# Attention and a routed expert layer on one core: when the first expert's weights are loaded and split, and at which steps two closings hand work to GpSimd

## The chip, the cores and the metric

The kernel runs on one core of a Trainium2 chip. The metric is the device time of one execution in microseconds (us). Engines are called by the profile's short names: PE (TensorE, matrix products), PEld (its weight loads), DVE (VectorE), ACT (ScalarE), POOL (GpSimd) and SP (SyncE, which only issues transfers here). Each engine works its own queue in program order and waits at semaphores for the others.

## The reference

The program computes an attention whose queries and keys may only meet inside the same hash bucket, and sends its result through a layer of eight experts:

```
x = bucket_attention(q, k, v, proj)            # 4 batches, 8 heads, 768 tokens, 64 wide -> 3072 tokens x 512
logits = x @ w_gate                            # 3072 x 8
for (token, e) in all pairs, highest logit first:
    if token is free and expert e has fewer than 384 tokens: assign it
for e in range(8):
    h = max(x[tokens of e] @ w1[e], 0)         # 384 x 512  by  512 x 1024
    out[tokens of e] = h @ w2[e]               # 384 x 1024 by 1024 x 512
```

The greedy assignment is done in rounds: each round finds which expert fills up next, and which 384 tokens it has. Such a round is a **closing**. There are eight; each yields one expert's tokens and the row numbers of its weights.

## The kernel before, in words

**Stages.** The first part (some 410 us) is the attention. Then closing 0 runs alone. From there on expert k's two matrix products run on PE while closing k+1 is worked in between, mostly on DVE, with short products on PE.

**Precision.** A weight or a token block is split into a high part (ACT copies it to a rounded format, `wh`, `xh`) and a low part (the difference, `wl`, `xl`). A product is three passes: high by high, weights' low by high, and high by the other low. So a weight piece is loaded by DMA to `wf`, copied by ACT to `wh` (L731), and subtracted by POOL to `wl` in two instructions of 128x512 (L743). A weight of an expert is four such pieces, so eight subtractions; both weights of an expert need sixteen. `wf`, `wh`, `wl` of each layer exist once.

**Steps.** `run` (L818) writes the expert part in 68 steps per expert. Steps 0 to 31 are the first layer: eight blocks `f` of four steps, three products of 384 columns to a step (L777), with ACT's `hh` (L779) and DVE's `hl` (L780) at the end of a block. Block f uses weight piece f//2, the low part from its fifth product on. Steps 32 to 67 are the second layer: three blocks `c` of twelve steps, two products of 512 columns to a step (L789); the last eight products of a block use `wl`, piece by piece, so that the second half of piece 3 is read by the last product of the block, in its last step (43 for the first block). Before a step, `run` emits what is planned for it: steps of the closing, splits of weights (`wsplit`, L725) and of tokens (`xsplit`, four times), loads, scatters of results. A step is only a place in each engine's program order; each engine reaches it at its own time. Steps of expert k are counted from 68k here and told from the expert's own step 0.

**Closings.** A closing is a generator (`phase`, L546), advanced at planned steps: lists E1 for closing 1 (over expert 0) and E2 for closing 2 (over expert 1), EV for the others. In E1 the entries are steps -12, -4, -3, 2, 6, 7, 8, 14, 20, 27, 33, 36, 39, 46; in E2 -9, -8, -6, 1, 8, 15, 20, 23, 27, 38, which is 59 to 106 counted from the start of expert 0. In order: the best logits and a compare; a count on PE and a threshold (L593 to L605); five more rounds of count (L518), threshold (L605 makes `d2`) and compare (L500); the outcome (L611 to L638, PE L614, L641); the member lists (L649, L677, L662 makes `cc`); the collection of the row numbers on PE (L651), and the update (L667 to L675). With the row numbers POOL gathers the tokens (`gather`, L709) by indirect DMA, and `wload` (L716) the weights.

**Hand-outs.** For experts 0 to 5 the subtractions of POOL are not emitted where the split is planned but put on a list (`pend`), with a step by which they must be emitted at the latest. At each closing step `step(p,n)` advances the closing, and `hand(n)` (L739) emits the next n of them behind a `tick` (L737), a copy of one element of the closing's latest result, so that POOL starts them only when DVE has got that far. The lists `hs` in `run` say how many at each closing step.

**Start.** `start` (L802) loads two pieces of expert 0's first weight, ends closing 0, gathers the tokens, splits pieces 0 and 1 (with DVE for the low parts) and the tokens. Then a tick on POOL waits for the tokens' split; behind it POOL issues the loads of pieces 2 and 3 and of the second weight in two halves. Their splits are planned in `run`: pieces 2 and 3 before steps 4 and 6 (`W10`), the second weight's before steps 9, 12, 15, 18 (`W20`).

Of the kernel before, what the change touches and what calls it, by code (L numbers as in the profile page):

```python
# [42 lines left out]
def attention(tc, nc, ctx, qT, kT, vv, proj, wg, x_dram, L, jp, identf, B, late=None, after=None):  # L43
# [322 lines left out]
    for t in range(6*NH+LAG+6):  # L366
        h,s=divmod(t,6)
        first=(t-LAG)%6==5
        if first: av(t)
        if t<6*NH and t not in early: ST(h,s,0)  # L370
        for x in S_at.get(t,[]): S_pass(*x)
        run(2*t)
        if h<NH: ST(h,s,1)
        if t>=1 and (t-1)//6<NH:
            hh,ss=divmod(t-1,6)
            lo(hh,ss,V if ss in (E0 if hh<1 else E1 if hh<2 else PAT[hh%2]) or t==6*NH else G_)
        run(2*t+1)
        if not first: av(t)
# [14 lines left out]
HS=[0,3,3,2,3,3,0,0,2,0]  # L393
BY=[-1,8,36]
W2=[2,4,7,11]
W10=[(2,4),(3,6)]
W20=[9,12,15,18]
XS=[57,57,60,63]
XS1=[61,61,64,65]
KW=[1,0,4,0,2,19,7,1]  # L400
# [1 line left out]
class Moe:  # L402
# [399 lines left out]
    def start(s):  # L802

        s.ps0=None; V=s.nc.vector
        s.wload(0,0,4,(0,1))
        next(s.ph0)
        s.gather(0)
        s.wsplit(0,0,0,V)
        next(s.ph0)
        s.ch=[s.phase(p) for p in range(8)]  # L810
        s.wsplit(0,0,1,V)
        s.xsplit0()

        s.gate=s.W[0,'x'][0][0:1,0,256:257].bitcast(F32); s.tick()
        s.wload(0,0,4,(2,3))
        s.wload(0,1,2)

    def run(s):  # L818
        V=s.nc.vector; ch=s.ch; at={}; NS=68
        def add(n,f,*a): at.setdefault(n,[]).append((f,a))  # L820
        def end(p):
            s.gather(p)
            if p<7: next(ch[p+1])
        def step(p,n):
            next(ch[p],None); s.hand(n)
        for p in range(1,8):
            b=NS*(p-1)
            ev=[b+e for e in (E1 if p==1 else E2 if p==2 else EV)]
            dec=ev[-3] if p<7 else ev[-2]-2
            hs=[0]*(len(ev)-10)+HS  # L830
            if p==1: hs=[0,0,0,0,0,2,2,2,2,2,0,1,1,0]
            if p==2: hs=[0,2,3,2,3,2,0,0,4,0]
            if p==7: ev=ev[-2:]; hs=[0,0]
            for e,n in zip(ev,hs): add(e,step,p,n)
            add(ev[-1],end,p)
            add(max(dec,b+WL[0]),s.wload,p,0); add(max(ev[-1],b+WL[1]),s.wload,p,1)
            for q in range(4):
                add(b+(W11 if p==1 else W1)[q],s.wsplit,p,0,q,None,b+NS+BY[0]+BY[1]*q if p<6 else 0)
                add(b+(XS1 if p==1 else XS)[q],s.xsplit,p,q)
        for k in range(8):  # L840
            for q in range(4): add(NS*k+(W2 if k else W20)[q],s.wsplit,k,1,q,None,NS*k+(BY[2] if k else 42) if k<6 else 0)
            for n in SC: add(NS*k+n,s.scatter)
        for q,n in W10: add(n,s.wsplit,0,0,q,None,8*q-2)
        for n in range(-NS,NS*8):
            for f,a in at.get(n,()): f(*a)
            while s.pend and s.pend[0][0]<=n: s.nc.gpsimd.tensor_tensor(*s.pend.pop(0)[1],op=ALU.subtract)
            if n<0: continue
            k,h=divmod(n,NS)
            if h<32: s.layer1(k,h//4,h%4)
            else: s.layer2(k,(h-32)//12,(h-32)%12)  # L850
        while s.late: s.scatter()
# [52 lines left out]
```

## Time and profile before

| | |
|---|---|
| time, median of 3 runs | 765.25 us (764.78 to 770.71) |
| the profiled execution | 768.65 us, its span in the trace 766.8 us |
| busy: PE, DVE, ACT, POOL | 698.3, 562.9, 403.2, 547.7 us |
| mean granted TensorE clock | 0.966 |
| GpSimd subtraction of a weight (L743) | 1278 ns, 92 of them |
| ScalarE copy of a weight piece (L731) | 1048 ns, 64 of them |

Busy PE is 91% of the span. The page's busy shares are an average over the attention, the lone closing and the experts, which have different limits; the change lies in the experts alone, so the rows further down are of that part. A time in the trace is counted from the span's start. Behind a row, `[3.94 <-POOL wl L743]` says that the engine sat idle for 3.94 us before it and what ended that.

### The profile page before, as it was taken

To read this page: it belongs to the slowest core of one execution; us is meant where nothing else is said; L and a number is where in the kernel's file an instruction comes from. 1 tells how busy PE (TensorE), PEld (TensorE's weight loads), DVE (VectorE), ACT (ScalarE), POOL (GpSimd) and SP (SyncE) were. 2 spreads that over 40 slices of the span, in tenths; PEclk is the share of its full clock that TensorE was granted. 3 is DMA by queue.
4 is the path that set the end of the run, shared out by engine and by line. 5 is a ranking of instruction groups with operands and counts; after the bars stand their busy time and mean duration, and the time that the engine had idled before them with its cause. 6 is when DMAs were issued, how large, how long until landed. Compare 5 with 4: busy or idle time off the path is not lost. (4 is left out here: it accounts for less than half of the span.)

```text
span 766.8 us, 19086 instructions
## 1 busy us (share of the span) xinstructions
PE 698.3 (91%) x7748; PEld 544.0 (71%) x7748; DVE 562.9 (73%) x1318; ACT 403.2 (53%) x788; POOL 547.7 (71%) x467
## 2 busy tenths in 40 slices
PE   7898898999999999998887687989999999999995
PEld 2566675767767676675665576877988888988894
DVE  6788978889888898987765687778888888843120
ACT  5776676777776777655562141614343434333430
POOL 7694969696886968765662375768787887887761
PEclk7899999999999999999997599999999999999998
DMA  8539655426454273420000343434262626262511
GB/s 206 147 96 220 149 157 123 121 74 166 129 122 123 80 190 98 105 58 23 22 22 23 97 166 111 165 138 151 86 217 77 227 67 237 59 244 97 207 39 42
DMA packets 40000, 93.57 MB, mean 122 GB/s; under 512 B 4597, under 2 KB 30569, under 8 KB 37865
## 3 DMA queue, kind: packets, MB, share of 16 engines
q1 hardware_dynamic: 33048, 46.21, 23.2%
q0 software_dynamic: 6784, 46.14, 17.2%
q8 instruction: 61, 1.00, 0.6%
q14 instruction: 27, 0.21, 0.1%
q10 hardware_dynamic: 80, 0.00, 0.0%
HBM read 59.53 MB, written 12.58 MB: 94 GB/s over the span
## 5 line engine op out<-in xcount | busy, mean ns | idle before, releaser
L258 POOL TENSOR_TENSOR lo<-pt 128x768 f16<-128x768 f32 x143 | 233.5, 1646 | 78.0 <-ACT pt L255 68.6
L255 ACT ACTIVATE pt<-pst 128x384 f32<-128x384 f32 x384 | 182.9, 491 | 98.6 <-PE pst L254 87.7
L231 DVE TENSOR_REDUCE m<-pss 128x1 f16<-128x770 f32 x192 | 182.6, 956 | 42.3 <-PE pss L229 41.3
L253 PE MATMUL pst<-qa,ka 128*128 128x384 f16 x384 | 125.6, 327 | 6.8 <-DVE XT L297 4.0
L254 PE MATMUL pst<-qb,kb 128*128 128x384 f16 x384 | 125.5, 327 | 1.1 <-DMA qb<-ql 1.1
L270 PE MATMUL psv<-vh,lo 128*128 128x65 f16 x1152 | 121.1, 194 | 1.8 <-POOL lo L258 1.8
L269 PE MATMUL psv<-vl,pt 128*128 128x64 f16 x1152 | 121.3, 193 | 0.0
L268 PE MATMUL psv<-vh,pt 128*128 128x65 f16 x1152 | 121.2, 194 | 0.0
L743 POOL TENSOR_TENSOR wl<-wf,wh 128x512 fp32r<-128x512 f32 x92 | 115.8, 1278 | 0.0
L268 PEld LDWEIGHTS <-pt 128*128 128x128 bf16 x1152 | 106.7, 98 | 12.7 <-issue 3.1
L269 PEld LDWEIGHTS <-pt 128*128 128x128 bf16 x1152 | 105.8, 99 | 9.5
L229 PE MATMUL pss<-ka,qa 128*128 128x385 f16 x384 | 95.4, 331 | 17.2 <-DVE m L231 14.6
L270 PEld LDWEIGHTS <-lo 128*128 128x128 f16 x1152 | 105.8, 97 | 2.0 <-POOL lo L258 1.9
L731 ACT CAST wh<-wf 128x1024 fp32r<-128x1024 f32 x64 | 65.1, 1048 | 38.3 <-DMA wf<-in_w_dram,zwidx 37.8
L779 ACT ACTIVATE hh<-ph 128x384 fp32r<-128x384 f32 x64 | 31.4, 491 | 83.3 <-PE ph L777 83.3
L229 PEld LDWEIGHTS <-qa 128*128 128x128 f16 x384 | 37.6, 98 | 50.4 <-issue 26.5
L780 DVE SCALAR_TENSOR_TENSOR hl<-ph,hh 128x384 fp32r<-128x384 f32 x64 | 35.3, 556 | 41.5 <-ACT hh L779 41.0
L777 PE MATMUL ph<-xh,wh 128*128 128x384 f32 x256 | 60.1, 349 | 3.3 <-DVE hl L780 3.0
L258 DVE TENSOR_TENSOR lo<-pt 128x768 f16<-128x768 f32 x49 | 61.6, 1258 | 1.5 <-ACT pt L255 1.0
L792 ACT COPY o<-po 128x512 f32<-128x512 f32 x24 | 14.1, 587 | 82.4 <-PE po L789 80.9
L777 PE MATMUL ph<-xl,wh 128*128 128x384 f32 x256 | 56.8, 340 | 0.0
L777 PE MATMUL ph<-xh,wl 128*128 128x384 f32 x256 | 56.1, 339 | 0.0
(263 smaller groups left out, 1418.1 us busy)
## 6 DMA issues: line engine op xcount, KB each, us to landing
vp<-in_vv_dram SPq DMA_DIRECT2D x8, 768.0 KB
x_dram<-X SPq DMA_DIRECT2D x16, 384.0 KB
qp<-in_qT_dram SPq DMA_DIRECT2D x7, 768.0 KB
kp<-in_kT_dram SPq DMA_DIRECT2D x7, 768.0 KB
qa<-qh SPq DMA_DIRECT2D x14, 192.0 KB
ka<-kh SPq DMA_DIRECT2D x14, 192.0 KB
qb<-qh SPq DMA_DIRECT2D x14, 192.0 KB
kb<-kh SPq DMA_DIRECT2D x14, 192.0 KB
```

The source lines that it names most:

```text
L229: T.matmul(ps[:,hf,0:HK],QA[u][:,j,qc*128:qc*128+128],KA[u][:,j,hf*HK:hf*HK+HK],start=True,stop=True)
L231: V.tensor_reduce(M6[h][:,qc:qc+1],ps[:,:,0:HK],axis=AX.XY,op=ALU.max,negate=True)
L253: T.matmul(ps[:,0:384],KA[u][:,j,kr],QA[u][:,j,r],start=True,stop=False)
L254: T.matmul(ps[:,0:384],KB[u][:,j,kr],QB[u][:,j,r],start=False,stop=True)
L255: A.activation(PT[h,kc][0][:,r],ps[:,0:384],AF.Exp,scale=0.125)
L258: eng.tensor_tensor(l,p,p.bitcast(BF)[:,1::2],op=ALU.subtract)
L268: T.matmul(av[:,c,:],ph[:,r],VH[u][:,j,kc,:],start=(kc==0 and c==0),stop=False,skip_group_check=True)
L269: T.matmul(av[:,c,0:64],ph[:,r],VL[u][:,j,kc,:],start=False,stop=False,skip_group_check=True)
L270: T.matmul(av[:,c,:],l[:,r],VH[u][:,j,kc,:],start=False,stop=False,skip_group_check=True)
L731: s.nc.scalar.copy(h[:,r],f[:,r])
L743: for _ in range(n): s.nc.gpsimd.tensor_tensor(*s.pend.pop(0)[1],op=ALU.subtract)
L777: T.matmul(p[:,0:384],a[:,o:o+128],b[:,d],start=n==0,stop=n==11)
```

## The change

The loads of pieces 2 and 3 of expert 0's first weight are issued by POOL straight behind the gather of its tokens, in front of the tick. Only the second weight's two halves stay behind the tick. The splits of pieces 2 and 3 move from steps 4 and 6 into `start`, behind the tokens' split; their subtractions go on the list with the same latest steps, 14 and 22. The splits of expert 0's second weight move three steps ahead each. The hand-outs of closing 1 and closing 2 get other numbers; their sums (12 and 16) stay.

```diff
-W10=[(2,4),(3,6)]
-W20=[9,12,15,18]
+W20=[6,9,12,15]
...
         s.gather(0)
+        s.wload(0,0,4,(2,3))
         s.wsplit(0,0,0,V)
...
         s.gate=s.W[0,'x'][0][0:1,0,256:257].bitcast(F32); s.tick()
-        s.wload(0,0,4,(2,3))
         s.wload(0,1,2)
+        s.wsplit(0,0,2,by=14)
+        s.wsplit(0,0,3,by=22)
...
-            if p==1: hs=[0,0,0,0,0,2,2,2,2,2,0,1,1,0]
-            if p==2: hs=[0,2,3,2,3,2,0,0,4,0]
+            if p==1: hs=[0,0,0,1,0,2,2,2,2,2,1,0,0,0]
+            if p==2: hs=[0,1,2,2,2,3,0,1,5,0]
...
-        for q,n in W10: add(n,s.wsplit,0,0,q,None,8*q-2)
```

## Rows read from the trace of the kernel before

**Rows 1.** Timeline of PE: first products of experts 0, 1, 2 and 3 (start, us, idle before)
```profile
442.10 0.96 PE L777 MATMUL ph<-xh,wh 128*128 128x384 f32 x4 [0.28 <-ACT xh L764]
...
490.26 0.69 PE L777 MATMUL ph<-xh,wh 128*128 128x384 f32 x3
...
533.96 0.88 PE L777 MATMUL ph<-xh,wh 128*128 128x384 f32 x4
...
572.71 0.88 PE L777 MATMUL ph<-xh,wh 128*128 128x384 f32 x4
```
**Rows 2.** Timeline of PE: two long waits, and the collection between them
```profile
474.44 0.50 PE L789 MATMUL po<-wl,hh 128*128 128x512 f32 x1 [3.94 <-POOL wl L743]
...
476.33 0.86 PE L651 MATMUL psa<-zRr,ohp 128*128 128x12 bf16 x24
...
504.20 0.32 PE L518 MATMUL psa<-zOH,zcmp 128*128 128x32 bf16 x6 [1.96 <-DVE zcmp L500]
```
**Rows 3.** Timeline of POOL: hand-outs of closings 1 and 2
```profile
464.62 2.52 POOL L743 TENSOR_TENSOR wl<-wf,wh 128x512 fp32r<-128x512 f32 x2
...
468.41 1.27 POOL L743 TENSOR_TENSOR wl<-wf,wh 128x512 fp32r<-128x512 f32 x1
...
473.14 1.25 POOL L743 TENSOR_TENSOR wl<-wf,wh 128x512 fp32r<-128x512 f32 x1
...
490.39 3.79 POOL L743 TENSOR_TENSOR wl<-wf,wh 128x512 fp32r<-128x512 f32 x3
...
499.75 3.75 POOL L743 TENSOR_TENSOR wl<-wf,wh 128x512 fp32r<-128x512 f32 x3
...
514.39 5.02 POOL L743 TENSOR_TENSOR wl<-wf,wh 128x512 fp32r<-128x512 f32 x4
```
**Rows 4.** Timeline of DVE: instructions beside POOL's subtractions, and one without
```profile
498.27 0.24 DVE L605 SCALAR_TENSOR_TENSOR zd<-zd,zn,zE 128x24 bf16<-128x24 bf16 x1
...
501.81 1.74 DVE L605 SCALAR_TENSOR_TENSOR zd<-zd,zn,zE 128x24 bf16<-128x24 bf16 x1
...
468.65 1.07 DVE L655 TENSOR_SCALAR zmi<-zpm 128x24 int32<-128x24 int32 x1
```
**Rows 5.** Windows: length, busy of PE/PEld/DVE/ACT/POOL, granted clock, DMA share, GB/s
```profile
432.00:435.00 3.00, 2.30 (x32) 1.99 (x29) 0.92 (x4) 0.90 (x1) 2.00 (x3) 0.50 0.81 258
...
474.00:477.00 3.00, 2.56 (x28) 1.82 (x29) 0.00 (x0) 0.58 (x1) 0.39 (x1) 0.66 0.98 421
477.00:480.00 3.00, 3.00 (x19) 2.51 (x16) 2.70 (x17) 0.96 (x2) 2.02 (x2) 0.77 0.20 55
...
504.00:507.00 3.00, 2.53 (x15) 2.23 (x15) 1.70 (x7) 0.00 (x0) 2.84 (x4) 0.78 0.00 0
507.00:510.00 3.00, 3.00 (x14) 2.86 (x13) 1.99 (x11) 0.49 (x1) 1.28 (x2) 0.65 0.23 87
```
**Rows 6.** Timeline of DVE and ACT after the start: the first rounds of closing 1
```profile
446.94 0.50 DVE L495 TENSOR_SCALAR zD<-zkey 128x24 int32<-128x24 int32 x5
448.08 0.17 DVE L593 TENSOR_SCALAR_CACHE_REDUCE zsat<-psa 128x8 bf16<-128x8 f32 x1 [0.65 <-PE ph L777]
...
448.71 1.05 ACT L731 CAST wh<-wf 128x1024 fp32r<-128x1024 f32 x1 [0.31 <-DMA wf<-in_w_dram,zwidx]
...
450.18 0.56 DVE L780 SCALAR_TENSOR_TENSOR hl<-ph,hh 128x384 fp32r<-128x384 f32 x1 [0.75 <-ACT hh L779]
```
**Rows 7.** Timeline of DVE and PE: the outcome of closing 1
```profile
466.93 0.25 DVE L620 SCALAR_TENSOR_TENSOR zwg<-zd,znn,zmxu 128x24 f32<-128x24 bf16 x1
...
468.06 0.20 PE L641 MATMUL psa<-zSTb,ntri 128*128 128x48 bf16 x1
```
**Rows 8.** Timeline of PE: first use of the tokens of expert 0 and of expert 1
```profile
437.55 1.12 PE L763 MATMUL px<-identf,xg 128*128 128x128 f32 x4 [1.84 <-DMA xg<-x_dram,zidx]
...
485.44 0.82 PE L751 MATMUL px<-identf,xg 128*128 128x128 f32 x6
```
**Rows 9.** Timeline of PEld: the last low piece of the second layer's first block, expert 1
```profile
519.47 0.19 PEld L789 LDWEIGHTS po<-wl,hh 128*128 128x128 f32 x1 [0.56 <-POOL wl L743]
```

## Prediction

> **What bounds the kernel now.** I first read the windows over the span: the attention is not touched, so I went to the expert part and looked in PE's timeline for each expert's first product [rows 1]. Expert 2 takes 572.71 - 533.96 = 38.75 us; expert 0 takes 48.2 and expert 1 43.7. So 9.4 and 4.9 us more than an expert needs lie in the two experts that the change touches, and nothing it does can be worth more than some 14 us. Next, the idle times of PE in these two: two waits stand out [rows 2]. At 474.44 PE has waited 3.94 us for the last low piece of the second layer's first block (POOL); at 504.20 it has waited 1.96 us for a compare of closing 2 (DVE). Then the windows behind both [rows 5]: the granted clock is 0.66 and 0.77 after the first, 0.78 and 0.65 after the second, that is, of its two levels (1.2 and 2.4 GHz) the lower one for more than half of these 3 us stretches. Each wait is paid twice.
>
> Who made PE wait? POOL's timeline [rows 3] shows the first: the last two low halves of expert 0's second weight were handed out behind the outcome and behind the member lists of closing 1 (468.41 and 473.14), though POOL had been free from 464.62 + 2.52 = 467.14. DVE's timeline shows the second [rows 4]: the instruction that makes `d2` takes 0.24 us, but 1.74 us at 501.81, when it ends at 503.55, right behind POOL's three subtractions (499.75 + 3.75 = 503.50). An instruction of this kind on DVE does not run beside POOL's subtractions. That is the thing to follow here: a subtraction handed out costs PE nothing by itself, but 1.25 us of DVE if it falls on such an instruction.
>
> **The change, part by part.** All working is on the profiled execution (768.65 us, span 766.8), which is 3.4 us above the median; I take the differences to the median, 765.25.
>
> *The last low piece.* In the new list for closing 1 the hand-outs are 1, 2, 2, 2, 2, 2, 1 at steps 2, 7, 8, 14, 20, 27, 33; each finds its pieces split by then, as the copies also move three steps ahead. The last one comes at step 33, behind POOL's pair that ends at 467.14 [rows 3]: with the tick and 1.27 for the subtraction it is done at about 468.6. PE comes to it at 474.44 - 3.94 = 470.5. The wait goes: **-3.9**. The clock behind it: (0.34 + 0.23) x 3 = 1.7 us lost [rows 5], less the 0.2 that lay in the wait: **-1.5**.
>
> *What that subtraction now lies beside.* Until now it held up L655 (1.07 us, until POOL's 468.41 + 1.27 [rows 4]), which leads to the lists and is not needed by PE before step 46. At 467.3 to 468.6 it lies beside the outcome, L620 to L638, whose first instruction at 466.93 is of the kind of L605 [rows 7]; and PE's L641 at 468.06 needs the flags at once. If DVE is held until 468.6, half a us of that work is left, and L641 comes at 469.2. Bounds: 0 (it gets between) and 1.3 (a whole subtraction). I take 1.1, since L655 and L605 were held to the end: **+1.1**.
>
> *The start.* POOL's loads of pieces 2 and 3 move into its idle time between gather and tick; ACT copies the pieces before the first `hh`. If piece 3 lands late, that `hh` is late; a cost of it is within the bounds below. A sure one lies in the one subtraction at step 2: it runs from about 446.8 to 448.1, where DVE has the five digits of L495 (0.50 us at 446.94 [rows 6]), integer operations like the held L655. The cover is the 0.65 us for which DVE waited before 448.08; held to 448.1, the digits end at 448.6. Of the 0.55 lost some comes back: DVE then waited 0.75 us for the second `hh`, which stood on ACT behind the copy of a piece that was still arriving (448.71), and now stands behind another copy of 1.05 us whose data should be there. Bounds: -0.75 (digits not held, that wait gone) and +1.3 (held by a whole subtraction). I take **+0.3**.
>
> *Expert 1's tokens.* The collection at 476.33 moves by -3.9 + 1.1 + 0.3 and by the part of the slow clock before it, (476.33 - 474.44) x 0.4 = -0.75: -3.3 us. Its row numbers start the gather, on POOL, in the same order as before. PE, at full clock, comes to the tokens (485.44 [rows 8]) 4.0 us sooner. There is no wait at 485.44, so how long they had been there isn't seen: 0 to 0.75, I take the middle, **+0.4**.
>
> *Closing 2's list* (before 2, 3, 2, 3, 2, 0, 0, 4, now 1, 2, 2, 2, 3, 0, 1, 5). At step 60 one instead of two: the second half of piece 0 is then subtracted at the next hand-out, which began at 490.39 [rows 3], so it is done at 491.65. PE, which began the expert at 490.26 [rows 1], needs it with the seventh product, some 1.2 to 1.3 us later: **+0.2** (0 to 1.3). At 62 two instead of three, at 76 two instead of three: POOL's row of 499.75 ends one subtraction sooner, and starts sooner by part of the one at 62. DVE's `d2` is then held 0 to 0.5 us instead of 1.5. PE's wait of 1.96 falls by 1.0 to 1.96; **-1.5**. With the long wait its clock loss goes, (0.22 + 0.35) x 3 less 0.1: **-1.6**. At 83 three instead of two: 3.8 us of POOL from step 88's count on, while the outcome's first instructions on DVE follow the count by some 2.9 us (an estimate: the count 0.32, three steps of up to 0.69 each [rows 1, 2], two short results), so they are held 0.9 us, of which PE's own products up to L641 hide all but **+0.3** (0 to 1.3).
>
> *Five at step 95.* Let T be step 88's count, 504.20 so far. The four subtractions behind the lists ran from T + 10.2 to T + 15.2 [rows 3], and PE waited 0.56 us for the last [rows 9], so it would have been ready at T + 14.7, with 1.6 us of slow clock in that. At full clock, and 0.3 later by the outcome, it is ready at T + 13.4. The lists: three subtractions hold the outcome until about T + 4.9, the one now handed out at 91 holds L655 until T + 6.5, and from L655 to the lists' end it took 3.3 us (469.7 to 473.0 at closing 1 [rows 3, 4]); five subtractions of 1.26 then end at T + 16.3. PE waits 2.9 us instead of 0.56: **+2.3**. Bounds: +1.0 (nothing held) and +2.7 (lists as late as now, T + 10.2).
>
> Sum: -3.9 - 1.5 - 1.5 - 1.6 = -8.5, and 0.3 + 1.1 + 0.4 + 0.2 + 0.3 + 2.3 = +4.6 given back: **-3.9**, so 765.25 - 3.9 = 761.3 us. Experts 2 to 7 run as they do, PE bound.
>
> The Trainium skill, page "SBUF — State Buffer", section "Who interferes with whom", says that VectorE and GpSimd contend for one shared pair of ports, taken for a whole instruction by whoever starts first, with VectorE operations that have two SBUF inputs or a two-port mode among those that need it. The trace agrees that they exclude each other, but not on the unit: `d2` at 501.81 sat out the rest of one subtraction and all of the next. What would follow if the unit were one instruction is the third rival.
>
> **The rivals.** *The clock falls again* behind the 2.9 us at step 95. For: it fell after 1.96 us. Against: this wait comes in three parts of about 1 us with a product between, as the pieces arrive one by one. Price 1.6: 762.9.
>
> *Nothing is given back*: DVE gets between POOL's subtractions, and the five come in time. For: `d2` at 498.27 took 0.24 us a moment after POOL's work; against: 1.74 and 1.07 [rows 4]. Then -8.5: 756.7.
>
> *DVE waits for one subtraction at most.* Then shortening a row from three to two takes only what is left of one: the 1.74 us would have been shorter with three, too, and the wait of 1.96 falls by 0.7 instead of 1.5: 762.1. The 1.74 speaks against it.
>
> *Slower: the weights delay the tokens.* At the start PE waits for the tokens (1.84 us [rows 8]); all of expert 0 and closing 1 stand behind them. Two pieces, 2 x 128 x 1024 x 4 bytes = 1.05 MB, now go out straight behind. If the transfer engines serve them beside or before the tokens, at 258 GB/s [rows 5] the last tokens come up to 4.1 us later, and the first products run at the low clock that PE had there (0.50 [rows 5]), another 1.6: 761.3 + 5.7 = 767.0. It turns the sign once tokens and clock together cost over 3.9. Against it: one queue, and the tokens issued first. The skill's "DMA: Bandwidth & Descriptors", section "Two DMAs through the same engine are not ordered", says that within one queue of an engine descriptors start in order; by that rule the tokens would not be late, and no run yet shows it.
>
> *All of it is given back*, each cost at its upper end: about 8.6 against 8.5, no change, 765.3. This is also what is seen if the copies come so late that the hand-outs wait in POOL.
>
> **How the numbers follow.** Forecast 0.50 (on its own 759.3 to 763.3), clock 0.20, nothing given back 0.13, one subtraction 0.04, slower 0.06, all given back 0.07. The range from 757.0 to 765.4 leaves out the better part of the third and the slower one. A change of under 1% (7.65 us) can't be told from none here: faster than 757.6 is only the case in which nothing is given back, 0.11; slower than 772.9 none reaches, 0.01.
>
> **What would show it.** PE's wait at the last product of the first block of expert 0 gone and the clock at 1.0 behind it; a new wait of about 1 us at L641 of closing 1; L605 of closing 2 at 0.24 to 0.7 us; a wait of 2 to 3 us for low pieces at the end of expert 1's first block; the first token transpose at 437.5 as before. It is wrong if DVE's outcome isn't held by the moved subtraction, if the tokens land later, or if the clock behaves otherwise behind short waits.

## The result, and the profile after

The changed kernel takes **760.13 us** (median of 8 runs, 758.0 to 761.77); the kernel before, on the same chip, 766.25 us (8 runs, 763.21 to 770.71). The ratio of the two times is 0.9908, 95% interval 0.9883 to 0.9932. The profiled execution took 760.15 us with a span of 758.1 us, against 768.65 and 766.8 before. The forecast was 761.3, from 757.0 to 765.4.

The two spans differ by 8.7 us, which is more than the 6.1 us between the medians. PE's timeline of the changed kernel, read at the same four places as [rows 1] (start, us, tile, form, count), shows why:

```profile
438.86 0.96 PE L776 MATMUL ph<-xh,wh 128*128 128x384 f32 x4 [0.28 <-ACT xh L763]
...
482.61 0.68 PE L776 MATMUL ph<-xh,wh 128*128 128x384 f32 x3
...
525.70 0.88 PE L776 MATMUL ph<-xh,wh 128*128 128x384 f32 x4
...
564.33 0.88 PE L776 MATMUL ph<-xh,wh 128*128 128x384 f32 x4
```

Expert 0's first product comes 3.24 us sooner, and all before it but the start is attention that the change does not touch. Over all traces of this study that product lay between 438.4 and 443.2 us, whatever the kernel; in two more traces of the changed kernel, unaltered, it stood at 441.41 and 443.21. So I count from it. (Up to the start, line numbers are one lower than before, from L396 on: L777 is now L776.) Expert 0 takes 43.75 us (48.16 before), expert 1 43.09 (43.70), expert 2 38.63 (38.75). Experts 0 and 1 gave 5.0 us, and everything behind them 0.4.

**The long wait is gone.** POOL's timeline, the hand-outs of closings 1 and 2 as in [rows 3]:

```profile
461.34 2.52 POOL L742 TENSOR_TENSOR wl<-wf,wh 128x512 fp32r<-128x512 f32 x2
463.95 1.28 POOL L742 TENSOR_TENSOR wl<-wf,wh 128x512 fp32r<-128x512 f32 x1
...
491.79 2.52 POOL L742 TENSOR_TENSOR wl<-wf,wh 128x512 fp32r<-128x512 f32 x2
495.26 3.77 POOL L742 TENSOR_TENSOR wl<-wf,wh 128x512 fp32r<-128x512 f32 x3
...
505.01 6.24 POOL L742 TENSOR_TENSOR wl<-wf,wh 128x512 fp32r<-128x512 f32 x5
```

The last low piece of the first block is made at 463.95, right behind the pair, and PE runs the eight products with `wl` in one row of 2.00 us at 466.63, without a wait. What is left of PE's waits in experts 0 and 1 stands in its timeline, as in [rows 2] and [rows 8]:

```profile
434.26 1.11 PE L762 MATMUL px<-identf,xg 128*128 128x128 f32 x4 [1.61 <-DMA xg<-x_dram,zidx]
...
437.51 0.67 PE L762 MATMUL psa<-identf,xg 128*128 128x128 f32 x4
...
465.77 0.20 PE L640 MATMUL psa<-zSTb,ntri 128*128 128x48 bf16 x1 [0.83 <-DVE zwidx L705]
...
466.63 2.00 PE L788 MATMUL po<-wl,hh 128*128 128x512 f32 x8
...
477.82 0.82 PE L750 MATMUL px<-identf,xg 128*128 128x128 f32 x6
...
495.31 0.32 PE L517 MATMUL psa<-zOH,zcmp 128*128 128x32 bf16 x6 [0.46 <-DVE zcmp L499]
...
508.83 0.50 PE L788 MATMUL po<-wl,hh 128*128 128x512 f32 x1 [0.27 <-POOL wl L742]
...
510.06 0.49 PE L788 MATMUL po<-wl,hh 128*128 128x512 f32 x1 [0.73 <-POOL wl L742]
...
511.30 0.50 PE L788 MATMUL po<-wl,hh 128*128 128x512 f32 x1 [0.74 <-POOL wl L742]
```

The 3.94 us have become 0.83 us at the outcome of closing 1; the 1.96 us at step 88 have become 0.46; the 0.56 us for the last low piece of expert 1 (a wait of PEld [rows 9]) have become three waits of PE, 1.74 us together. DVE's timeline shows what stands behind each, as in [rows 4, 6, 7]:

```profile
443.70 1.47 DVE L494 TENSOR_SCALAR zD<-zkey 128x24 int32<-128x24 int32 x5
...
446.91 0.56 DVE L779 SCALAR_TENSOR_TENSOR hl<-ph,hh 128x384 fp32r<-128x384 f32 x1 [0.48 <-ACT hh L778]
...
463.95 1.32 DVE L621 TENSOR_TENSOR asg<-asg,zwg 128x24 f32<-128x24 f32 x1
...
494.42 0.24 DVE L604 SCALAR_TENSOR_TENSOR zd<-zd,zn,zE 128x24 bf16<-128x24 bf16 x1
...
498.19 0.88 DVE L619 SCALAR_TENSOR_TENSOR zwg<-zd,znn,zmxu 128x24 f32<-128x24 bf16 x1
...
506.52 4.75 DVE L666 TENSOR_SCALAR zbnd<-wt,zcm 128x8 f32<-128x8 f32 x1
```

Lay these beside POOL's rows: L621 starts with POOL's subtraction at 463.95 and ends with it at 465.2; L619 ends at 499.07, POOL's three at 499.03; L666 ends at 511.27, POOL's five at 511.25. `d2` (L604) is clear of the two at 491.79, which end at 494.31.

The clock, in windows as in [rows 5] (busy of PE, PEld, DVE, ACT, POOL; granted clock; DMA share; GB/s), behind the place of the old 3.94 us, around step 88, and behind the three waits:

```profile
469.00:472.00 3.00, 3.00 (x37) 2.42 (x36) 2.56 (x16) 0.26 (x1) 1.11 (x1) 1.00 0.95 396
...
495.00:498.00 3.00, 2.42 (x18) 2.13 (x19) 1.90 (x8) 0.38 (x1) 3.00 (x4) 1.00 0.00 0
498.00:501.00 3.00, 3.00 (x19) 2.84 (x19) 2.97 (x14) 0.58 (x2) 2.83 (x4) 1.00 0.09 34
511.00:514.00 3.00, 2.71 (x12) 2.25 (x13) 2.93 (x18) 2.12 (x3) 2.35 (x3) 1.00 0.24 52
```

It is 1.00 throughout, at the higher of its two levels (2.4 GHz), where the first trace of the kernel before had 0.66 and 0.78.

### The profile page after: what moved, and what is told of

The parts are those of the page before. It is cut to its first block, busy times and chain, and to the rows that moved or that the text cites. A ratio compares the mean times of both kernels' runs of the same rounds, so it can differ in the third digit from the quotient of the medians.

```text
span 758.1 us, 19094 instructions
## 1 busy us (share of the span) xinstructions
PE 693.3 (91%) x7748; PEld 540.6 (71%) x7748; DVE 565.0 (75%) x1318; ACT 403.8 (53%) x788; POOL 547.6 (72%) x468
## 5 line engine op out<-in xcount | busy, mean ns | idle before, releaser
L776 PE MATMUL ph<-xh,wh 128*128 128x384 f32 x256 | 59.9, 348 | 3.0 <-DVE hl L779 2.7
L776 PE MATMUL ph<-xl,wh 128*128 128x384 f32 x256 | 56.0, 337 | 0.0
L776 PE MATMUL ph<-xh,wl 128*128 128x384 f32 x256 | 55.8, 337 | 0.0
```

Of the source, the lines that this page charges most:

```text
L776: T.matmul(p[:,0:384],a[:,o:o+128],b[:,d],start=n==0,stop=n==11)
```

## The experiments

Stage lengths below are from first product to first product in PE's timeline (E0, E1: experts 0 and 1), times are medians beside runs of the kernel before on the same chip. My theory: both long waits were POOL's order of work and DVE held behind it. The rivals: the weights' arrival, one held instruction at most per subtraction, and chance of the clock.

**The start alone** (changed kernel with both old lists):

```diff
-            if p==1: hs=[0,0,0,1,0,2,2,2,2,2,1,0,0,0]
-            if p==2: hs=[0,1,2,2,2,3,0,1,5,0]
+            if p==1: hs=[0,0,0,0,0,2,2,2,2,2,0,1,1,0]
+            if p==2: hs=[0,2,3,2,3,2,0,0,4,0]
```

> The changed start (loads of pieces 2 and 3 ahead of the tick, their copies in the start, the second weight's splits three steps sooner) with both lists as before. Theory: what PE waited for is the last hand-out behind the member lists at step 39, not the arrival of weights, so the wait of 3.9 us stays, expert 0 lasts 48 us within 0.7, and the time is that of the kernel before within 0.8. Rival (earlier weights are what counts): expert 0 loses 3 us or more.

Measured: 765.53 us, ratio 0.9971 (0.9942 to 0.9999), E0 48.98, E1 44.04. That is 1.1 us below the kernel before beside it (766.65) where at most 0.8 was expected, and expert 0 is 0.3 us above its range; neither is the 3 us of the rival. PE's timeline still has the wait:

```profile
473.17 0.80 PE L788 MATMUL po<-wl,hh 128*128 128x512 f32 x1 [3.92 <-POOL wl L742]
```

Bringing the weights forward gives next to nothing by itself: the last low piece was late for its place in POOL's order, not for its data.

**Closing 1's list alone** (kernel before with the new list for closing 1):

```diff
-            if p==1: hs=[0,0,0,0,0,2,2,2,2,2,0,1,1,0]
+            if p==1: hs=[0,0,0,1,0,2,2,2,2,2,1,0,0,0]
```

> The kernel before with closing 1's new hand-outs alone (1, 2, 2, 2, 2, 2, 1 at steps 2, 7, 8, 14, 20, 27, 33). Nothing is split yet at step 2, so the list runs one behind and its last item comes out at its latest step, 42, behind POOL's load for expert 1. Theory: the last subtraction then ends about 472.2 in the times of the kernel before, PE waits 1 to 2 us for it instead of 3.9, and the time falls by 2.5 to 4 us. Rival (without the sooner start the list brings nothing): within 0.8 us of the kernel before.

Measured: 763.23 us, 0.9945 (0.9913 to 0.9976), E0 46.92. The time fell by 3.4 us, as expected, but not through a shorter wait for the last low piece: in PE's timeline the 3.9 us are gone altogether, and two waits of 1.1 us at the outcome and at the collection have come:

```profile
466.85 0.20 PE L641 MATMUL psa<-zSTb,ntri 128*128 128x48 bf16 x1 [1.07 <-DVE zwidx L706]
...
471.99 0.79 PE L651 MATMUL psa<-zRr,ohp 128*128 128x12 bf16 x24 [1.09 <-DVE zRr L677]
```

With the old start the list brings part of the gain; in the traces E0 comes to 43.75 (44.28 and 44.33 in later traces) only with both. Which part of the start the list needs, the loads in front of the tick or the splits three steps sooner, no run separates.

**Start and closing 1's list, closing 2's old list:**

```diff
-            if p==2: hs=[0,1,2,2,2,3,0,1,5,0]
+            if p==2: hs=[0,2,3,2,3,2,0,0,4,0]
```

> The changed kernel, but with closing 2's hand-outs as before (0, 2, 3, 2, 3, 2, 0, 0, 4, 0). Theory: the change's parts lie in different stages and add up; the start and closing 1's list give expert 0 its 4.4 us (wait of 3.9 and low clock of 1.5 gone, 1.0 given back at the outcome), so expert 0 lasts 43.8 us, expert 1 again 43.7 (a wait of about 2 us at step 88 and low clock behind it), in all 4 to 5 us below the kernel before. Rival (the two lists hang together, since expert 1 starts sooner against its loads): expert 1 gets longer than 43.7 by a us or more, and the gain is below 3.5.

Measured: 760.23 us, 0.989 (0.9843 to 0.9937), E0 44.28, E1 42.14: the time of the whole change, and 6.4 us below the kernel before beside it where 4 to 5 were expected. The interval overlaps that of the run before (closing 1's list alone). PE's timeline and the windows around step 88:

```profile
501.08 0.32 PE L517 MATMUL psa<-zOH,zcmp 128*128 128x32 bf16 x6 [1.92 <-DVE zcmp L499]
```
```profile
501.00:504.00 3.00, 2.65 (x19) 2.36 (x20) 1.86 (x10) 0.00 (x0) 2.84 (x4) 1.00 0.00 0
504.00:507.00 3.00, 3.00 (x20) 2.84 (x19) 2.47 (x16) 0.81 (x2) 1.68 (x2) 1.00 0.25 93
```

The wait is the one of [rows 2], but this time the clock behind it did not fall, against 0.78 and 0.65 in [rows 5].

**Closing 2's list alone** (kernel before with the new list for closing 2, the reverse of the lines above):

> The kernel before with closing 2's new hand-outs alone (0, 1, 2, 2, 2, 3, 0, 1, 5, 0). Theory: expert 0 stays at 48.2 us; in expert 1 the wait at step 88 falls from 2.0 to about 0.5 and the clock stays up (2.7 us gained up to the outcome), but the five subtractions behind the lists cost 2.1 at the first block's end, so 0.3 to 1.0 us are gained. Rival (the new list is worth what its removed wait was, 3.5): expert 1 lasts 40 us, 3 to 4 us gained.

Measured: 768.79 us, 1.0017 (0.999 to 1.0045), E0 49.18, E1 44.27. The wait at step 88 is 0.45 us, the three for low pieces at the end of the block 0.30, 0.73 and 0.72, and in this trace the clock fell behind them (0.56 and 0.87 in two stretches of 3 us). The 0.3 to 1.0 us that were expected did not come: closing 2's list trades one wait for another and is worth nothing that can be measured. With the run above it: **the whole gain is the start and closing 1's list together.**

**Three subtractions at step 76 again** (changed kernel):

```diff
-            if p==2: hs=[0,1,2,2,2,3,0,1,5,0]
+            if p==2: hs=[0,1,2,2,3,2,0,1,5,0]
```

> The changed kernel with three instead of two subtractions at step 76 and two instead of three at step 83. Theory (DVE's instruction that makes `d2` sits out all back-to-back subtractions of POOL): the row at 76 takes 3.8 us instead of 2.5 again, `d2` of the round before step 88 takes 1.2 to 1.8 us instead of 0.24, PE's wait at step 88 is 1.2 to 2.0 us instead of 0.46, and the outcome's first instruction at step 88 is back at about 0.25 us instead of 0.88. Expert 1 takes 1 to 2.5 us longer than the changed kernel's 43.1 to 43.4, the upper end if the clock falls behind the wait. Rival (DVE waits for what is left of one subtraction at most): `d2` at most 0.7 us, PE's wait below 0.9 us, expert 1 as long as in the changed kernel within 0.5 us.

Measured (one run): 766.35 us, with 767.52 us in one run of the kernel before beside it; E1 43.72, against 43.09, 43.38 and 43.04 in three traces of the changed kernel. DVE's, POOL's and PE's timelines:

```profile
499.19 1.18 DVE L604 SCALAR_TENSOR_TENSOR zd<-zd,zn,zE 128x24 bf16<-128x24 bf16 x1
...
503.89 0.23 DVE L619 SCALAR_TENSOR_TENSOR zwg<-zd,znn,zmxu 128x24 f32<-128x24 bf16 x1
```
```profile
496.56 3.77 POOL L742 TENSOR_TENSOR wl<-wf,wh 128x512 fp32r<-128x512 f32 x3
```
```profile
501.02 0.32 PE L517 MATMUL psa<-zOH,zcmp 128*128 128x32 bf16 x6 [1.39 <-DVE zcmp L499]
...
515.16 0.50 PE L788 MATMUL po<-wl,hh 128*128 128x512 f32 x1 [0.68 <-POOL wl L742]
...
516.51 0.50 PE L788 MATMUL po<-wl,hh 128*128 128x512 f32 x1 [0.84 <-POOL wl L742]
```

`d2` ends at 500.37, POOL's third subtraction at 500.33, and PE pays 1.39 us: the third subtraction of that row is the price of step 88. `d2` began at 499.19, when only the third was left (497.84 to 499.09 was the second), so this run doesn't tell whether `d2` waits for one subtraction or for the whole row; at 1.18 us it lies a little below the 1.2 to 1.8 expected and clear of the rival's 0.7. The stage grew by 0.3 to 0.7 us only, less than the 1 to 2.5 expected: the clock stayed at 1.00, and of the three waits at the end of the block the first is gone.

**Closing 2: 2, 3, 2, 2, 3, 0, 1, 3** (changed kernel; three at 62 and three at 95, where the whole change has two and five, and two instead of one at 60):

```diff
-            if p==2: hs=[0,1,2,2,2,3,0,1,5,0]
+            if p==2: hs=[0,2,3,2,2,3,0,1,3,0]
```

> The changed kernel with closing 2's list as 0, 2, 3, 2, 2, 3, 0, 1, 3, 0: two subtractions come out earlier, at steps 60 and 62, and three instead of five stand behind the lists. Theory: what the list costs is where a subtraction meets DVE. At 60 a second one fits (DVE reaches the next d2 3.4 us after the hand-out's tick, two take 2.5); at 62 a third one holds d2 by 0.7 us, which DVE spends waiting for hh just after (1.04 us) anyway; with three behind the lists PE's waits for low pieces (2.1 us) go. Expert 1 lasts 41.0 us, 2 us below the changed kernel. Rival (the earlier ones only move the wait): d2 of step 62 and the one after come later, PE waits 1 us more at steps 76 to 88, expert 1 stays above 42.3.

Measured: 760.44 us, 0.9911 (0.9878 to 0.9944), E0 44.06, E1 41.20. The waits for low pieces are gone, step 88 waits 1.10 us. In the traces this is some 2 us less of expert 1; in the time it does not show.

**The last subtraction of closing 1 on DVE** (changed kernel; behind the outcome DVE makes it itself):

```diff
-            if p==1: hs=[0,0,0,1,0,2,2,2,2,2,1,0,0,0]
+            if p==1: hs=[0,0,0,1,0,2,2,2,2,2,0,-1,0,0]
...
-            next(ch[p],None); s.hand(n)
+            next(ch[p],None)
+            if n<0: V.tensor_tensor(*s.pend.pop(0)[1],op=ALU.subtract)
+            else: s.hand(n)
```

> The changed kernel with the subtraction that closing 1 hands out at step 33 done by DVE instead, at step 36 behind the outcome. Theory: POOL's subtraction beside the outcome is what holds L621 for 1.32 us and makes PE wait 0.83 us at L640; with it gone the wait goes, DVE pays 0.7 us (its price for 128x512 in the start) in front of the lists, which PE needs only at the collection: expert 0 lasts 43.0 us, 0.8 less, or up to 0.4 less if the collection then waits. Rival (DVE was late for another reason): PE's wait at L640 stays, expert 0 lasts 44 us or more.

Measured: 761.93 us, 0.9918 (0.9884 to 0.9952), E0 43.59, E1 44.14. PE's and DVE's timelines:

```profile
466.70 0.20 PE L640 MATMUL psa<-zSTb,ntri 128*128 128x48 bf16 x1
```
```profile
466.69 0.67 DVE L827 TENSOR_TENSOR wl<-wf,wh 128x512 fp32r<-128x512 f32 x1
```

PE's wait at the outcome is gone, and DVE takes 0.67 us for what POOL takes 1.27. Expert 0 lasts 0.7 us less than in the two traces of the changed kernel in which the clock was low early in expert 0, as here (44.28 and 44.33). Nothing of it is left in the time: expert 1 lost a microsecond in this trace, where the clock fell behind the three waits for low pieces:

```profile
512.09:515.09 3.00, 2.78 (x7) 2.20 (x8) 2.93 (x19) 1.90 (x3) 2.27 (x3) 0.50 0.26 57
```

**Both of these together**, and the changed kernel unaltered beside them:

> Both edits together on the changed kernel. Theory: they lie in different stages and add up: expert 0 43.0, expert 1 41.0, together 84.0 against 86.8 in the changed kernel, and 756 to 758 us of time. Rival: the two disturb each other or lie in the noise, 760 as the changed kernel.

> The changed kernel once more, unaltered. Theory: after a wait of some 2 us the clock sometimes falls and sometimes not (the same early stretch of expert 0 had it low in four of six traces), which moves a trace by 1 to 2 us: in this trace either the early stretch or the one behind the low pieces of expert 1 is at the low clock with an even chance, and expert 0 and 1 together last 86.8 to 88.5 us. Rival (the clock follows from the program alone): both stretches at full clock as in the first trace, 86.8.

Measured: 758.05 us with both (6 runs, 755.09 to 760.54), 0.9877 (0.9827 to 0.9928), E0 43.13 and E1 40.82; 761.40 us unaltered (12 runs), 0.9916 (0.9886 to 0.9946), E0 44.33 and E1 43.38. As the intervals overlap, a second time, again with 6 and 12 runs:

> The changed kernel with both further edits (closing 2: two subtractions at step 62 moved, closing 1: its last subtraction on DVE) a second time, with more runs. Theory (3.0 to 3.5 us less than the changed kernel in experts 0 and 1, from the first pair of profiles: 83.95 against 86.84 and 87.71 us): 1 to 4 us below the changed kernel of the same call, so 756 to 759.5 us where that is at 760 to 761.5; experts 0 and 1 together 83.5 to 85.5 us in the trace, the lower end if the clock does not fall behind the first product. Rival (what they take away is given back outside, or the first time was chance): within 0.7 us of the changed kernel.

> The changed kernel, unaltered, beside it. Both theories: 760 to 762 us, 0.988 to 0.994 of the kernel before; experts 0 and 1 together 86.8 to 88 us.

Measured: **755.83 us** with both (6 runs, 754.35 to 757.84), 0.9852 (0.9811 to 0.9893), E0 43.37 and E1 40.58; 760.88 us unaltered (12 runs, 757.08 to 766.0), 0.9914 (0.988 to 0.9948), E0 44.28 and E1 43.04. That is 3.4 us below the changed kernel the first time and 5.1 the second, with 3.8 and 3.4 us in experts 0 and 1. This version is faster than the kernel before by its intervals. Against the changed kernel the medians and the traces say the same both times, but the two intervals overlap by a little. Alone, neither edit showed in the time; E0 and E1 of the one with closing 2's list summed to 85.26 and of the one with DVE's subtraction to 87.73.

**The kernel before, unaltered, a second profile:**

> The kernel before, unaltered, a second profile. Theory (the clock behind waits of some 2 us, and 6 to 12 us behind the first product, differs from execution to execution): the waits of 3.9 us at the end of expert 0's first block and of 1.9 to 2.0 us at step 88 stand again; expert 0 takes 48 to 49.5 us and expert 1 42.2 to 44.5, where a granted clock under 0.85 in the stretch 6 to 12 us behind expert 0's first product adds 0.5 to 1 us to the 48.2. Rival (the clock there belongs to the changed start): the granted clock is 0.95 or more in that stretch, as in the first profile of the kernel before, and expert 0 takes 48.2 us within 0.3.

Measured (one run): 767.43 us, E0 50.29, above the 48 to 49.5 expected, E1 42.55. From 6 to 12 us behind expert 0's first product the granted clock was 1.00, as the rival had it, but expert 0 did not stay at the rival's 48.2, and the two other kernels with the old start had the low clock there (below). PE's timeline and the windows behind its two waits:

```profile
472.86 0.80 PE L789 MATMUL po<-wl,hh 128*128 128x512 f32 x1 [3.94 <-POOL wl L743]
...
504.19 0.32 PE L518 MATMUL psa<-zOH,zcmp 128*128 128x32 bf16 x6 [1.92 <-DVE zcmp L500]
...
518.21 0.50 PE L789 MATMUL po<-wl,hh 128*128 128x512 f32 x1 [0.31 <-POOL wl L743]
```
```profile
472.86:475.86 3.00, 3.00 (x29) 2.19 (x30) 0.00 (x0) 0.59 (x1) 0.00 (x0) 0.50 0.96 410
475.86:478.86 3.00, 3.00 (x15) 2.42 (x12) 2.73 (x17) 1.28 (x2) 2.05 (x2) 0.50 0.22 49
478.86:481.86 3.00, 3.00 (x13) 2.37 (x13) 2.69 (x11) 0.71 (x1) 2.39 (x3) 0.87 0.69 203
...
504.00:507.00 3.00, 2.53 (x19) 2.25 (x20) 1.86 (x8) 0.00 (x0) 2.84 (x4) 1.00 0.00 0
```

The same two waits as in [rows 2], to 0.04 us, and other clocks behind them: (0.5 + 0.5 + 0.13) x 3 = 3.4 us lost behind the first instead of 1.7, nothing behind the second instead of 1.7.

## Why the prediction was right, step by step

| step | predicted | measured |
|---|---|---|
| wait for the last low piece | -3.9 | gone |
| clock behind it | -1.5 | 1.00; the loss before was 1.7 in one trace, 3.4 in the other |
| outcome of closing 1 held | +1.1 | +0.98 |
| start | +0.3 | 0 in the changed kernel's first trace |
| expert 1's tokens | +0.4 | 0 |
| second half of piece 0 | +0.2 | 0, no wait |
| wait at step 88 | -1.5 | 1.96 to 0.46: -1.5 |
| clock behind it | -1.6 | 1.00; before, a loss in one trace of two |
| outcome of closing 2 held | +0.3 | 0, held 0.64 us but no wait of PE |
| five at step 95 | +2.3 | +2.0 |

*Expert 0.* The wait, its clock and the held outcome came as worked out. The outcome was held at L621 and not at L620, from 0.18 to 1.32 us, to the subtraction's end; from the small product ahead of it to L640 it took 2.59 us instead of 1.61. Without that subtraction on POOL, L640 does not wait (the run with it on DVE). The start cost nothing: the digits (L494) were held, 1.47 us for five instead of 0.50 [rows 6], but DVE had spare time ahead of the second `hh` (0.48 us of wait instead of 0.75), and from the first product to the second small outcome product it took 24.32 us against 24.35.

*Expert 1.* `d2` at 0.24 us and three subtractions instead of two bringing 1.18 back are the mechanism itself. POOL's five end 15.9 us behind step 88's count (505.01 + 6.24 - 495.31), where the working had 16.3. From that count to the block's last product PE now takes 511.30 - 495.31 = 15.99 us, in the later two traces of the changed kernel 16.08 and 15.94; in the second trace of the kernel before, where the clock stayed up there too, it took 518.21 - 504.19 = 14.02. The waits that PE shows for low pieces are 1.74 us, less than the 2 to 3 that I gave as a sign: the rest of the 2.0 us lies in products that run one by one, each 0.50 us, instead of in a row. I had the outcome of closing 2 delay PE by 0.3; L619 was held, but PE had products of its own until the flags came, and L640 shows no wait there. The tokens of expert 1 were there in time although PE came to them sooner.

*The sum.* Experts 0 and 1 together took 91.86 and 92.84 us in two traces before, and 86.84, 87.71 and 87.32 in three after: -5.1 us between the means, where the sum had -3.9. By expert, the terms add up to -3.6 for expert 0 (the tokens are taken up before its end) and -0.3 for expert 1; the means differ by -5.1 and by 0.0 us. So what was gained lies in expert 0, as the runs with closing 2's list left as it was and with that list alone say as well. The mechanisms were right and their signs too; what was off is the size of what is given back, 3.0 us in the table instead of 4.6: the start, the tokens, the half piece and the second outcome were costed at 1.2 together and cost nothing in the first trace, and the two larger terms were some 0.4 too high together. The two clock terms were read from one trace, and the second gives other values: 3.4 us instead of 1.7 behind the first wait, and none instead of 1.7 behind the second. That both traces come to 3.4 us in all, close to the 3.1 forecast, is luck. Behind expert 1 the means differ by another 0.6 us, so the traces place 5.7 of the 6.1 us between the medians; the rest I can't name, and the interval's near end, 0.68% of 766 or 5.2 us, doesn't ask for it. Nor is it all insight that 760.13 us lies 1.2 from the forecast time: the change took 6.1 us where 3.9 were forecast, and the kernel before came out at 766.25 us in 8 runs instead of the 765.25 that I counted from.

*The rivals.* "Slower: the weights delay the tokens" fell. PE's wait for the first tokens is 1.61 us where it was 1.84 [rows 8], but that wait was over at 434.26, and POOL turned to the first of the two loads only at 433.83. What tells is the last tokens, which PE transposes after both loads have been issued. PE's row for them in the kernel before, and POOL's first load in the changed kernel:

```profile
440.80 0.62 PE L763 MATMUL psa<-identf,xg 128*128 128x128 f32 x4
```
```profile
433.83 0.94 POOL L721 DMA_INDIRECT wf<-in_w_dram,zwidx  x1 [0.30 <-issue]
```

The last tokens are transposed 3.25 us behind the first ones in both (440.80 - 437.55 and 437.51 - 434.26), without a wait, and the first product comes 4.60 us behind the first ones where it was 4.55, though 1.05 MB of weights were issued straight behind the tokens. The Trainium skill, "DMA: Bandwidth & Descriptors", section "Two DMAs through the same engine are not ordered", has descriptors of one queue start in order within an engine; the 3.25 us agree with it, though the order itself is not seen in a row. "All given back" fell too: the hand-outs of closing 1 did not wait for copies, in none of the three traces. "Nothing is given back" holds for none of the large terms. "DVE waits for one subtraction at most" fell for `d2`: in five traces with three in a row it started within the second and ended with the third. "The clock falls again" did not happen in the first trace of the changed kernel, nor in the two later ones, but it did in the two other kernels that have the same three waits; I had it at 0.20 with a price of 1.6, and two in five would have been nearer.

One thing was not foreseen: in the changed kernel's first trace DVE waited 1.04 us for an `hh` at 488.33, because ACT had two copies of weights (from 485.92, 1.99 us) ahead of it. The copy before them had started late, behind 0.76 us of waiting for one of POOL's subtractions (484.16). PE did not pay for it.

## What to carry to other kernels

Ask of a low-priority piece of work first in which order its engine meets it, and only then when its data arrive: bringing the weights forward gave next to nothing (1.1 us) until the list used it, and in the traces the list alone gave only a part. When work is moved between slots of a shared schedule, follow for each slot which instruction of the other engine lies beside it; closing 2's list took 1.5 us of waiting from step 88 and put 2.0 us more at the end of the block. Split a small gain by stages counted from a common event, and look at a second profile of the same kernel, before a difference of 1 or 2 us in one trace is put down to a change.

## What the runs showed of the hardware

**The clock behind the same waits differs from execution to execution.** Behind waits of 3.9 us it fell in four traces of four; behind waits of 1.9 to 2.3 us at step 88 in three of five (in the kernel before once yes, once no); behind the two or three waits for low pieces, each under 0.9 us, in two of six. There is also a stretch from 6 to 12 us behind expert 0's first product: in 11 of 14 traces the granted clock fell there, in two of four with the old start and nine of ten with the new one, with no wait of PE above 0.82 us in the products ahead. What these traces share lies earlier: in the 3 us ahead of the first product, where PE comes out of its wait for the tokens, the granted clock was 0.50 to 0.63 in the eleven and 0.70 to 0.72 in the three in which it then stayed up, so there it had risen sooner. Why it did is open. Windows of the changed kernel's first trace, and of the second of the same program:

```profile
444.86:447.86 3.00, 2.17 (x17) 1.86 (x17) 2.08 (x12) 2.94 (x8) 1.90 (x3) 1.00 0.66 273
```
```profile
447.41:450.41 3.00, 2.37 (x14) 1.87 (x14) 2.08 (x12) 2.93 (x8) 1.90 (x3) 0.65 0.68 281
```

In the next 3 us it was 1.00 and 0.78. Within expert 0, PE's waits ahead of it are the same in both (0.41 and 0.81 us the longest), and E0 is 43.75 in the one and 44.33 in the other.

**Who goes first between two subtractions is not fixed either.** DVE's and POOL's timelines of the second trace of the changed kernel, at the update of closing 2:

```profile
509.64 1.03 DVE L666 TENSOR_SCALAR zbnd<-wt,zcm 128x8 f32<-128x8 f32 x1
510.59 1.33 DVE L667 TENSOR_SCALAR zug<-zwg 128x24 f32<-128x24 f32 x1
...
511.91 1.43 DVE L669 TENSOR_TENSOR Lm<-Lm,zbnd 128x192 f32<-128x192 f32 x1
513.26 1.24 DVE L670 TENSOR_TENSOR un<-un,zug 128x24 f32<-128x24 f32 x1
```
```profile
508.12 6.34 POOL L742 TENSOR_TENSOR wl<-wf,wh 128x512 fp32r<-128x512 f32 x5
```

Here L666 got in after the subtraction that it met, and three of those behind it after one more each; in the first trace the same instruction waited 4.75 us through four ends, and 4.72 us in the third. Each of the instructions that I saw held ends with some subtraction; whether with the first or the last differed between executions for the update, while `d2` was held to the last in all five traces in which it met more than one. Over all experts of the 14 traces `d2` met a subtraction 196 times, and each time it ended 0.04 to 0.17 us behind the last of POOL's row. The Trainium skill's page "SBUF — State Buffer", section "Who interferes with whom", gives one whole instruction as the unit for which one of the two has the shared ports; the second trace agrees (1.03 to 1.43 us, about one subtraction each), the first does not (4.75 us).
